# K and V in four transfers of 4 MB each, two heads per softmax, weights in the K and V buffers

## The chip, the cores and the metric

The kernel runs on one core of a Trainium2 chip. The metric is the device time of one execution in microseconds (us); the median of several runs counts.

## The reference

One decode step: attention of two tokens over a cached window, times a gate from a small dense network, plus the input. Cut to what matters:

```python
# x (2,1,448); k_cache, v_cache (2,8,8192,256); wq (448,4096); wo (4096,448)
# w1 (448,1792); w2 (1792,448); all bf16
W = 2048                                    # the last 2048 positions
xn = layernorm(x)
q = (xn @ wq) as 16 heads of 256            # two query heads for each K/V head
k, v = k_cache[:, :, -W:], v_cache[:, :, -W:]   # 8 heads, repeated twice
p = softmax(q k^T / 16)
s = (p v, heads side by side) @ wo
g = silu(relu(xn @ w1) @ w2)
return x + s * g
```

## The kernel before

Almost all bytes are K and V: 8 heads, each 2 MB of K and 2 MB of V for both batches, 33.5 of 44.1 MB. They come in sixteen transfers, one for a head's K or V: partition p = 2i + b holds 32 positions of batch b, a row of 32 x 256 values or 16 KB in one piece (`kv_src`, L175). wq (3.7 MB), w1 and w2 (1.6 MB each) come ahead of them, wo (3.7 MB) after them, in pieces of 16, 11, 4 and 1 of its 32 j-slices.

The program lists instructions by hand for each engine (`_Prog.op`, `_Prog.dma`); an instruction waits for those named in its `deps`, and each engine works through its own list in order. All the large transfers stand in the list of the sync engine (SP), so that one whose buffer is not free holds up those behind it. There are three buffers for K, three for V, two for the transposed K (`kt`), and own buffers for the weights (`wqo` for wq and later wo, `w1_sb`, `w2_sb`). `pump` (L504) puts a load into SP's list as soon as the step that frees its buffer has been listed.

A head k goes through these steps:

- `do_qbd`: POOL puts the head's queries into a block layout, four copies.
- `do_T(k, c)`, c = 0 to 3: VectorE (DVE) transposes a quarter of K in blocks of 32x32 words (L344).
- `do_S(k, c)`: TensorE (PE) multiplies that quarter with the queries, four matmuls of 512 columns into the bank `sbk`; at c = 0 a matmul of `wrow` with `wcol` first fills the bank with a large negative mask.
- the chain of the softmax: `ch_max` (DVE, the maximum of each row), `ch_rmT` (PE, transposes it), `ch_mrow` (DVE, the maximum over the rows of a query, negated), `ch_bias` (PE), `ch_bsb` and `ch_exp` (ScalarE, ACT), `ch_pt` (DVE, transposes the weights), `ch_sum` (PE) and `ch_rs` (DVE, 1/sum).
- `do_PV(k, q)`, q = 0 to 3: PE, 16 matmuls of 512 columns with V, four at a time side by side; `do_osb` (ACT) scales by 1/sum; `do_oT` (PE) and `do_at` (DVE) put the result into place.

The lists are written as a software pipeline (L441 to L471): the T and S of head k are interleaved with the chain of head k - 1 and the PV of head k - 2. After the last head its chain and the last three PV follow. Ahead of all this stand `do_q` (queries from wq), `do_H`, `do_hT` and `do_F` (the dense network; its gate `do_gate` after the T of head 0). At the end `at2` (L538) is made, and 32 x 4 matmuls with wo follow (L541), waiting at the first j of each piece for its landing; then two operations on DVE and the transfer of the output.

PE's matmuls are recorded by one helper, so L253 stands for nearly all of them; they are told apart by their tiles (`sbk` scores, `obk` PV and q, `fbk` the dense network and wo).

Of the kernel before, what the change touches and what calls it, by code (L numbers as in the profile page):

```python
# [74 lines left out]
def bass_recurrent_scan__sliding_block_cached__dense_activation_relu__decode_kernel(  # L75
# [31 lines left out]
    QW = 16 + 8 * 128  # L107
# [3 lines left out]
    with es:  # L111
# [19 lines left out]
        fold16 = named("fold16", [128, 16], BF)  # L131
# [19 lines left out]
        rm = [named(f"rm{i}", [128, 1], F32) for i in range(2)]  # L151
        mrow = [named(f"mrow{i}", [128, 128], F32) for i in range(2)]
# [3 lines left out]
        rs = named("rs", [128, NPAIR], F32)  # L156
# [4 lines left out]
        wqo = named("wqo", [128, 32 * D], BF)  # L161
        assert SLOTS * HC <= 32 * D
# [20 lines left out]
        last_T, last_PV = {}, {}  # L183
# [12 lines left out]
        d_wq = pr.dma(SP, wqo[:, 0:SLOTS * HC], wq_src)  # L196
        d_w1 = pr.dma(SP, w1_sb[:, :], w1_src)
        d_w2 = pr.dma(SP, w2_sb[:, :].rearrange("p (hf f) -> p hf f", hf=2), w2_src)
# [10 lines left out]
        p_mr = [pr.op(POOL, lambda e, t=t: e.memset(t[0:1, :], 0.0)) for t in mrow][-1]  # L209
        p_wr = pr.op(POOL, lambda e: e.memset(wrow[0:2, :], 0.0))  # L210
# [11 lines left out]
        for e2 in range(2):  # L222
# [10 lines left out]
            view(wrow, 0, [[16, 8], [2, 2], [1, 2]], n=2), view(ident, 0, [[0, 8], [1, 2], [0, 2]], n=2)), [p_wr, p_id])  # L233
        v_wc = pr.op(DVE, lambda e: e.tensor_scalar(
            out=view(wcol, 0, [[2, 256], [1, 2]], n=2), in0=view(ident, 0, [[0, 256], [1, 2]], n=2),
# [9 lines left out]
        def fold16_op(e):  # L245
            with nc.allow_low_precision("zeros and ones"):
                return e.tensor_reduce(out=fold16[:, :], in_=view(ident, 0, [[1, 16], [16, 8]]), axis=AX.X, op=ALU.add)
        v_f16 = pr.op(DVE, fold16_op)
        v_gs = pr.op(DVE, lambda e: e.tensor_copy(
            view(gsum, 0, [[4, 32], [1, 4]]), view(fold16, 0, [[0, 32], [1, 4]])), [v_f16])  # L250
# [14 lines left out]
        def do_q():  # L265
            deps = [d_wq, v_xr, a_z[0]]
            for s in range(SLOTS):
                for i in range(4):
                    lo = s * HC + i * 512
                    o = pr.op(PE, mm(obk[0][32 * i:32 * i + 4, :], xr[:, 4 * s:4 * s + 4], wqo[:, lo:lo + 512],  # L270
                                     s == 0, s == SLOTS - 1, tile_position=(0, 32 * i)), deps)
                    deps = []
            st["q_mm"] = o
            for par in range(2):
                v = pr.op(DVE, lambda e, par=par: e.tensor_scalar(  # L275
                    out=view(kt[1], 128 * par, [[256, 8], [32, 4], [1, 32]]),
                    in0=view(obk[0], par, [[64, 8], [0, 4], [2, 32]]),
                    scalar1=SCALE, scalar2=None, op0=ALU.mult), [o])
            st["osb", -2] = v
            deps = [v, p_id]  # L280
            for h in range(2):
                for cp in range(8):
                    n = 8 * h + cp
                    o = pr.op(PE, mm(nbk[:, 16 * n:16 * n + 16], kt[1][:, 128 * n:128 * n + 128],
# [7 lines left out]
        def do_qbd(k):  # L292
            deps = [st["qall"], p_qz, st.get(("S", k - 2))]
            for a in range(4):
                st["qbd", k] = pr.op(POOL, lambda e, a=a: e.tensor_copy(  # L295
                    view(qbd[k % 2], 16 + 32 * a, [[2, 2], [128, 8], [1, 2]], n=32, p0=32 * a),
                    view(qall, 32 * k, [[16, 2], [2, 8], [1, 2]], n=32, p0=32 * a)), deps)
                deps = []

        def do_H(u):  # L300
            deps = [d_w1, a_z[2], st.get("fbk"), st.get("h_n")]
            for s in range(SLOTS):
                lo = s * FC + u * (FC // 2)
                o = pr.op(PE, mm(fbk[0:4, 0:FC // 2], xr[:, 4 * s:4 * s + 4], w1_sb[:, lo:lo + FC // 2],
# [14 lines left out]
        def do_F():  # L319
            deps = [d_w2, st["hT"]]  # L320
            for f in range(14):
                for i in range(4):
                    lo = f * D + i * NCOL
                    o = pr.op(PE, mm(fbk[32 * i:32 * i + 17, 0:NCOL], h_sb[:, f:f + 17],
                                     w2_sb[:, lo:lo + NCOL],
# [15 lines left out]
        def do_T(k, c):  # L341
            src, dst = words(kbuf[k % NKB]), words(kt[k % 2])
            deps = [d_k[k], st.get(("S", k - 2)), st["qT"]] if c == 0 else []
            st["T", k, c] = pr.op(DVE, lambda e: e.transpose(  # L344
                view(dst, 32 * c, [[128, NT], [1, 32]]), view(src, 32 * c, [[128, NT], [1, 32]])), deps)
            if c == 3:
                last_T[k] = st["T", k, c]

        def do_S(k, c):
            bank, t = sbk[k % 2], kt[k % 2]  # L350
            if c == 0:
                pr.op(PE, mm(bank[:, :], wrow[0:2, :], wcol[0:2, :], True), [v_wr, v_wc, st.get(("exp", k - 2))])
            deps = [st["T", k, c]] + ([st["qbd", k]] if c == 0 else [])
            for par in range(2):
                for h in range(2):
                    w = 16 + (2 * c + par) * 128 - 16 * h
                    st["S", k] = pr.op(PE, mm(bank[:, :], qbd[k % 2][:, w:w + 128],
                                              view(t, 256 * h + 64 * c + par, [[512, NT // 2], [2, 32]]),
                                              False, c == 3 and par == 1 and h == 1), deps)
                    deps = []  # L360

        def ch_max(k):
            st["rm", k] = pr.op(DVE, lambda e: e.tensor_reduce(  # L363
                out=rm[k % 2][:, :], in_=sbk[k % 2][:, :], axis=AX.X, op=ALU.max),
                [st["S", k], st.get(("rmT", k - 2))])
# [6 lines left out]
        def ch_mrow(k):  # L372
            st["mrow", k] = st["mbk"] = pr.op(DVE, lambda e: e.tensor_reduce(  # L373
                out=view(mrow[k % 2], 0, [[16, 8], [1, 4]], n=1), in_=view(mbk, 0, [[0, 8], [1, 4], [16, 8]], n=1),
                axis=AX.X, op=ALU.max, negate=True), [st["rmT", k], p_mr, st.get(("bias", k - 2))])
# [14 lines left out]
        def ch_pt(k):  # L390
            st["pt", k] = pr.op(DVE, lambda e: e.transpose(pt[k % 2][:, :], e_sb[k % 2][:, :]),  # L391
                                [st["exp", k], last_PV.get(k - 2)])
# [8 lines left out]
        def do_PV(k, q):  # L401
            bank, src, p = obk[k % 2], vbuf[k % NVB], pt[k % 2]
            deps = [d_v[k], st["pt", k], a_z[1], st.get(("osb", k - 2))] if q == 0 else []
            for n in range(4 * q, 4 * q + 4):
                i = n % 4
                st["PV", k] = pr.op(PE, mm(bank[32 * i:32 * i + 20, :], p[:, 32 * n:32 * n + 20],
                                          src[:, 512 * n:512 * n + 512],
                                          q == 0, q == 3, tile_position=(0, 32 * i)), deps)
                deps = []
            if q == 3:  # L410
                last_PV[k] = st["PV", k]

        def do_osb(k):
            st["osb", k] = pr.op(ACTE, lambda e: e.activation(  # L414
                o_sb[k % 2][:, :], obk[k % 2][:, :], ACT.Copy, scale=rs[:, k:k + 1]),
                [last_PV[k], st["rs", k], st.get(("oT", k - 2))])

        def do_oT(k):
            deps = [st["osb", k], v_fold, st["nbk"]]
            for dhi in range(2):  # L420
                for t2 in range(2):
                    lo = 256 * t2 + 128 * dhi
                    o = pr.op(PE, mm(nbk[:, 4 * dhi:4 * dhi + 4], o_sb[k % 2][:, lo:lo + 128],
                                     fold[:, 16 * t2:16 * t2 + 4], dhi == 0 and t2 == 0, dhi == 1 and t2 == 1), deps)
# [3 lines left out]
        def do_at(k):  # L428
            for b in range(2):
                st["at", k] = st["nbk"] = pr.op(DVE, lambda e, b=b: e.tensor_tensor(  # L430
                    out=view(at_exp, 128 * b + 16 * k, [[4, 2], [8, 2], [1, 4]]),
                    in0=view(nbk, 2 * b, [[4, 2], [1, 2], [0, 4]]),
                    in1=view(qmask, 0, [[0, 2], [0, 2], [1, 4]]), op=ALU.mult), [st["oT", k], v_qm])

        steps = []

        def add(fn, *a):
            if 0 <= a[0] < NPAIR:
                steps.append((fn, a))

        for k in range(NPAIR):  # L441
            c, p, o = k - 1, k - 2, k - 3
            add(do_qbd, k)
            add(do_T, k, 0)
            add(ch_max, c)
            add(do_S, k, 0)
            add(ch_rmT, c)
            add(do_T, k, 1)
            add(ch_mrow, c)
            add(do_oT, o)  # L450
            add(do_at, o)
            add(do_T, k, 2)
            if k < NPAIR - 1:
                add(do_PV, p, 0)
            add(do_S, k, 1)
            add(ch_bias, c)
            add(ch_bsb, c)
            add(ch_exp, c)
            if k < NPAIR - 1:
                add(do_PV, p, 1)  # L460
            add(do_T, k, 3)
            add(do_S, k, 2)
            if k < NPAIR - 1:
                add(do_PV, p, 2)
            add(ch_pt, c)
            add(ch_sum, c)
            add(ch_rs, c)
            add(do_S, k, 3)
            if k < NPAIR - 1:
                add(do_PV, p, 3)  # L470
                add(do_osb, p)  # L471
        x, y, z = NPAIR - 3, NPAIR - 2, NPAIR - 1
# [113 lines left out]
```

## Time and profile before

| | |
|---|---|
| median of 3 runs | 111.65 us (111.58 to 112.1) |
| the profiled execution, its own time | 111.46 us |
| its span in the profile | 110.2 us |
| HBM read | 44.11 MB, 400 GB/s over the span |
| busy, share of the span | PE 64%, DVE 57%, PE weight loads 26%, ACT 17%, POOL 9% |
| mean granted TensorE clock | 0.864 |

Rows of the timeline read: start in us from the span's start, duration in us, engine, line, operation, output<-inputs, shapes, count, and in brackets how long the engine was idle before and what ended that. In section 2 of the page each digit is one fortieth of the span (2.755 us), in tenths.

### The profile page before, as it was taken

The page shows a single profiled execution, that of the slowest core. Times are in us where ns is not written, and L with a number is a line of the kernel's source. Part 1 is how long each engine was busy: PE and PEld are TensorE (multiplying, and loading weights), DVE is VectorE, ACT ScalarE, POOL GpSimd, SP SyncE. Part 2 cuts the span into 40 slices and gives each one's busy share as a digit, 9 for nine tenths or more (in the row PEclk, how much of TensorE's full clock was granted, in tenths as well). Part 3 has the DMA queues.
Part 4 walks back from the last instruction along what each step waited for, and adds up shares of the span by engine and source line. Part 5 has one row for each costly group of instructions (what it writes and reads, how often), then busy time and mean ns, then how long its engine had stood idle before and what let it go on. Part 6 is the DMA issues. An engine that isn't in the chain of part 4 may idle for free.

```text
span 110.2 us, 1454 instructions
## 1 busy us (share of the span) xinstructions
PE 70.2 (64%) x594; PEld 28.4 (26%) x594; DVE 63.3 (57%) x107; ACT 18.7 (17%) x40; POOL 10.2 (9%) x48
## 2 busy tenths in 40 slices
PE   0010746759948509994994895399979977834551
PEld 0000203134213202332331341133234432321540
DVE  2164057249999248739943990785499996221001
ACT  2970000000003000221032032003103220602000
POOL 6700000500020200011002002000200000000000
PEclk9999998599999965699579999655999999997555
DMA  6898999999999999999999999999999999999940
GB/s 167 354 480 356 433 410 461 428 434 428 422 428 434 422 434 422 434 422 437 411 428 422 434 422 434 422 434 422 434 422 434 411 440 416 440 419 416 406 162 1
DMA packets 3473, 44.19 MB, mean 401 GB/s; under 512 B 394, under 2 KB 524, under 8 KB 908
## 3 DMA queue, kind: packets, MB, share of 16 engines
q1 hardware_dynamic: 3440, 44.11, 94.8%
q8 instruction: 4, 0.07, 0.2%
q10 hardware_dynamic: 28, 0.01, 0.0%
q14 instruction: 1, 0.01, 0.0%
HBM read 44.11 MB, written 0.00 MB: 400 GB/s over the span
## 4 chain that ended last, share of the span: by engine, by line
DMA 63%; PE 19%; DVE 14%; SPq 2%; issue 1%
DMA kbuf<-in_A_k_cache_dram 37%; DMA wqo<-in_A_wo_dram 16%; DMA wqo<-in_A_wq_dram 10%; DVE kt L344 8%; PE sbk L253 6%; PE fbk L253 6%; PE obk L253 5%; DVE kt L275 2%; SPq L36 2%; DVE h_n L307 1%; PE nbk L253 1%; DVE rm L363 1%; PE mbk L253 1%; DVE tmp L549 0%; DVE h_sb L316 0%
## 5 line engine op out<-in xcount | busy, mean ns | idle before, releaser
L253 PE MATMUL sbk<-kt,qbd 128*128 128x512 bf16 x128 | 37.8, 422 | 14.7 <-DVE kt L344 14.5
L344 DVE STREAM_TRANSPOSE kt<-kbuf 128x1024 f32<-128x1024 f32 x32 | 38.3, 1218 | 11.2 <-DMA kbuf<-in_A_k_cache_dram 11.2
L253 PEld LDWEIGHTS sbk<-kt,qbd 128*128 128x128 bf16 x128 | 11.0, 106 | 32.1 <-DVE kt L344 20.8
L295 POOL COPY qbd<-qall 32x32 bf16<-32x32 bf16 x32 | 6.5, 204 | 68.8 <-PE sbk L253 53.1
L253 PE MATMUL obk<-vbuf,pt 128*20 128x512 bf16 x128 | 11.9, 410 | 1.5 <-DMA vbuf<-in_A_v_cache_dram 1.5
L382 ACT ACTIVATE bias<-mbk 128x1 f32<-128x1 f32 x8 | 1.4, 170 | 43.2 <-PE mbk L253 43.2
L414 ACT ACTIVATE o_sb<-obk,rs 128x512 bf16<-128x512 f32 x8 | 5.5, 686 | 18.5 <-PE obk L253 18.5
L391 DVE STREAM_TRANSPOSE pt<-e_sb 128x512 bf16<-128x512 bf16 x8 | 5.5, 683 | 3.0 <-ACT e_sb L386 3.0
L386 ACT ACTIVATE e_sb<-sbk,bias 128x512 bf16<-128x512 f32 x8 | 5.5, 687 | 0.3
L363 DVE TENSOR_REDUCE rm<-sbk 128x1 f32<-128x512 f32 x8 | 5.3, 657 | 0.5 <-PE sbk L253 0.5
L275 DVE TENSOR_SCALAR kt<-obk 128x1024 bf16<-128x1024 f32 x2 | 2.4, 1220 | 5.3 <-PE obk L253 5.3
L253 PE MATMUL obk<-wqo,xr 128*4 128x512 bf16 x28 | 3.2, 624 | 3.5 <-DMA wqo<-in_A_wq_dram 3.5
L253 PE MATMUL mbk<-ident,xg 2*128 2x2 bf16 x7 | 0.3, 163 | 7.9 <-DVE xg L223 7.9
L430 DVE TENSOR_TENSOR at_exp<-nbk,qmask 128x16 bf16<-128x16 f32 x16 | 1.9, 158 | 5.8 <-PE nbk L253 5.8
L253 PE MATMUL fbk<-wqo,at 128*17 128x112 bf16 x128 | 3.4, 296 | 2.9 <-DMA wqo<-in_A_wo_dram 2.9
L253 PEld LDWEIGHTS obk<-vbuf,pt 128*20 128x20 bf16 x128 | 2.9, 89 | 7.5 <-issue 4.9
L253 PE MATMUL fbk<-w_sb,xr 128*4 128x448 bf16 x14 | 4.2, 460 | 0.7 <-DVE h_n L307 0.7
L253 PEld LDWEIGHTS mbk<-one_f,mrow 1*128 1x128 f32 x16 | 2.9, 224 | 4.6 <-DVE kt L344 2.5
L373 DVE TENSOR_REDUCE mrow<-mbk 1x32 f32<-1x256 f32 x8 | 3.1, 386 | 1.3 <-PE mbk L368 1.3
L549 DVE TENSOR_TENSOR tmp<-fbk,g_sb 128x112 f32<-128x112 f32 x1 | 0.3, 273 | 6.1 <-PE fbk L253 6.1
L253 PEld LDWEIGHTS fbk<-wqo,at 128*17 128x17 bf16 x128 | 2.8, 129 | 3.3 <-issue 1.8
L253 PE MATMUL mbk<-one_f,mrow 1*128 1x1 f32 x16 | 3.5, 288 | 0.0
(64 smaller groups left out, 44.5 us busy)
## 6 DMA issues: line engine op xcount, KB each, us to landing
kbuf<-in_A_k_cache_dram SPq DMA_DIRECT2D x8, 2048.0 KB, 21.5
vbuf<-in_A_v_cache_dram SPq DMA_DIRECT2D x8, 2048.0 KB, 18.6
wqo<-in_A_wq_dram SPq DMA_DIRECT2D x1, 3584.0 KB, 11.0
w_sb<-in_B_w_dram SPq DMA_DIRECT2D x2, 1568.0 KB, 16.0
wqo<-in_A_wo_dram SPq DMA_DIRECT2D x1, 1792.0 KB, 15.7
wqo<-in_A_wo_dram SPq DMA_DIRECT2D x1, 1232.0 KB, 18.0
wqo<-in_A_wo_dram SPq DMA_DIRECT2D x1, 448.0 KB, 18.6
wqo<-in_A_wo_dram SPq DMA_DIRECT2D x1, 112.0 KB, 18.4
```

The source lines that it names most:

```text
L36: o = _Op(eng, lambda e: e.dma_start(dst, src), [d for d in deps if d is not None], True)
L253: return lambda e: e.matmul(out_ap, lhsT=lhsT, rhs=rhs, start=start, stop=stop, skip_group_check=True, **kw)
L275: v = pr.op(DVE, lambda e, par=par: e.tensor_scalar(out=view(kt[1], 128 * par, [[256, 8], [32, 4], [1, 32]]), in0=view(obk[0], par, [[64, ...
L295: st["qbd", k] = pr.op(POOL, lambda e, a=a: e.tensor_copy(view(qbd[k % 2], 16 + 32 * a, [[2, 2], [128, 8], [1, 2]], n=32, p0=32 * a), view ...
L344: st["T", k, c] = pr.op(DVE, lambda e: e.transpose(view(dst, 32 * c, [[128, NT], [1, 32]]), view(src, 32 * c, [[128, NT], [1, 32]])), deps)
L363: st["rm", k] = pr.op(DVE, lambda e: e.tensor_reduce(out=rm[k % 2][:, :], in_=sbk[k % 2][:, :], axis=AX.X, op=ALU.max), [st["S", k], st.ge ...
L373: st["mrow", k] = st["mbk"] = pr.op(DVE, lambda e: e.tensor_reduce(out=view(mrow[k % 2], 0, [[16, 8], [1, 4]], n=1), in_=view(mbk, 0, [[0, ...
L382: st["bsb", k] = st["mbk"] = pr.op(ACTE, lambda e: e.activation(bias[k % 2][:, :], mbk[:, 128:129], ACT.Copy), [st["bias", k]])
L386: st["exp", k] = pr.op(ACTE, lambda e: e.activation(e_sb[k % 2][:, :], sbk[k % 2][:, :], ACT.Exp, bias=bias[k % 2][:, 0:1], accum_out=ssum ...
L391: st["pt", k] = pr.op(DVE, lambda e: e.transpose(pt[k % 2][:, :], e_sb[k % 2][:, :]), [st["exp", k], last_PV.get(k - 2)])
L414: st["osb", k] = pr.op(ACTE, lambda e: e.activation(o_sb[k % 2][:, :], obk[k % 2][:, :], ACT.Copy, scale=rs[:, k:k + 1]), [last_PV[k], st[ ...
L430: st["at", k] = st["nbk"] = pr.op(DVE, lambda e, b=b: e.tensor_tensor(out=view(at_exp, 128 * b + 16 * k, [[4, 2], [8, 2], [1, 4]]), in0=vi ...
```

## The change

- K and V come in four transfers each of 4 MB: heads k and k + 4 of both batches. Partition p = 4i + g holds 64 positions of one of the four, a row of 32 KB.
- There are two buffers for K, two for V and one `kt`. wq lies in the second V buffer, w1 and w2 in the first, wo goes into the first K buffer once round 2 has been transposed. `load_v(0)` waits for the last matmul of `do_F`, `load_v(1)` for that of q, wo for `T(2, 7)`.
- A round k has eight T and eight S steps (of the same size as before; `c, gh = divmod(e, 2)`), one softmax for the two heads, and 32 PV matmuls. With one `kt`, `T(k, e)` waits for `S(k-1, e)`.
- `ch_mrow` has a second DVE operation; `do_qbd` has eight copies on POOL, `do_at` four products on DVE.
- The list's order is plainer: the T and S of rounds 0 and 1, with the chain of round 0 between those of round 1; then `chain(1, 0)` (the chain of round 1 with the PV of round 0 in it), T and S of round 2, `chain(2, 1)`, T and S of round 3, `chain(3, 2)`, PV of round 3.
- wo comes in pieces of 17, 9, 4 and 2.

The core of the diff:

```diff
-    NT = W // 64
+    NT = W // 32
-    NPAIR = HKV
+    NQ = HKV // 2
-    NKB = 3
-    NVB = 3
-    WO_PARTS = [16, 11, 4, 1]
+    WO_PARTS = [17, 9, 4, 2]
...
-        wqo = named("wqo", [128, 32 * D], BF)
-        w1_sb = named("w1_sb", [128, SLOTS * FC], BF)
-        w2_sb = named("w2_sb", [128, 14 * D], BF)
-        kbuf = [named(f"kbuf{i}", [128, ROW], BF) for i in range(NKB)]
-        vbuf = [named(f"vbuf{i}", [128, ROW], BF) for i in range(NVB)]
-        kt = [named(f"kt{i}", [128, ROW], BF) for i in range(2)]
+        kbuf = [named(f"kbuf{i}", [128, ROW], BF) for i in range(2)]
+        vbuf = [named(f"vbuf{i}", [128, ROW], BF) for i in range(2)]
+        kt = named("kt", [128, ROW], BF)
+        wq_sb, w12, wo_sb = vbuf[1], vbuf[0], kbuf[0]
...
         def kv_src(k, cache):
-            return cache[:, k, SK - W:SK, :].rearrange("b (i t) d -> i b (t d)", t=NT)
+            return cache.rearrange("b h s d -> (b h) s d")[k::NQ, SK - W:SK, :].rearrange("g (i t) d -> i g (t d)", t=NT)
...
         def load_k(k):
-            d_k[k] = pr.dma(SP, kbuf[k % NKB][:, :], kv_src(k, A_k_cache), [last_T.get(k - NKB)])
+            d_k[k] = pr.dma(SP, kbuf[k % 2][:, :], kv_src(k, A_k_cache), [st.get(("T", k - 2, 7))])
         def load_v(k):
-            d_v[k] = pr.dma(SP, vbuf[k % NVB][:, :], kv_src(k, A_v_cache), [last_PV.get(k - NVB)])
+            d_v[k] = pr.dma(SP, vbuf[k % 2][:, :], kv_src(k, A_v_cache),
+                            [(st["F"], st["q_mm"])[k] if k < 2 else st["PV", k - 2]])
...
-        def do_T(k, c):
-            src, dst = words(kbuf[k % NKB]), words(kt[k % 2])
-            deps = [d_k[k], st.get(("S", k - 2)), st["qT"]] if c == 0 else []
-            st["T", k, c] = pr.op(DVE, lambda e: e.transpose(
-                view(dst, 32 * c, [[128, NT], [1, 32]]), view(src, 32 * c, [[128, NT], [1, 32]])), deps)
+        def do_T(k, e):
+            c, gh = divmod(e, 2)
+            src, dst = words(kbuf[k % 2]), words(kt)
+            lo = 128 * (NT // 2) * gh + 32 * c
+            deps = [st.get(("S", k - 1, e))] + ([d_k[k], st["qT"]] if e == 0 else [])
+            st["T", k, e] = pr.op(DVE, lambda e: e.transpose(
+                view(dst, lo, [[128, NT // 2], [1, 32]]), view(src, lo, [[128, NT // 2], [1, 32]])), deps)
...
         def ch_mrow(k):
-            st["mrow", k] = st["mbk"] = pr.op(DVE, lambda e: e.tensor_reduce(
-                out=view(mrow[k % 2], 0, [[16, 8], [1, 4]], n=1), in_=view(mbk, 0, [[0, 8], [1, 4], [16, 8]], n=1),
-                axis=AX.X, op=ALU.max, negate=True), [st["rmT", k], p_mr, st.get(("bias", k - 2))])
+            v = st["mbk"] = pr.op(DVE, lambda e: e.tensor_reduce(
+                out=mx8[k % 2][0:1, :], in_=view(mbk, 0, [[1, 8], [8, 16]], n=1),
+                axis=AX.X, op=ALU.max, negate=True), [st["rmT", k]])
+            st["mrow", k] = pr.op(DVE, lambda e: e.tensor_copy(
+                view(mrow[k % 2], 0, [[8, 16], [1, 8]], n=1), view(mx8[k % 2], 0, [[0, 16], [1, 8]], n=1)),
+                [v, st.get(("bias", k - 2))])
...
+        def chain(k, pv=None):
+            ch_max(k)
+            ch_rmT(k)
+            ch_mrow(k)
+            ch_bias(k)
+            ch_bsb(k)
+            ch_exp(k)
+            if pv is not None:
+                for q in range(8):
+                    do_PV(pv, q)
+                do_osb(pv)
+            ch_pt(k)
+            ch_sum(k)
+            ch_rs(k)
+            if pv is not None:
+                do_oT(pv)
+                do_at(pv)
+
+        load_k(0)
+        load_k(1)
         do_q()
         do_H(0)
         do_H(1)
         do_hT()
         do_F()
+        load_v(0)
+        do_qbd(0)
+        do_qbd(1)
+        for e in range(8):
+            do_T(0, e)
+            do_S(0, e)
+            if e == 4:
                 do_gate()
+        load_k(2)
+        load_v(1)
...
+        load_k(3)
+        chain(1, 0)
+        load_v(2)
+        do_qbd(2)
+        for e in range(8):
+            do_T(2, e)
+            do_S(2, e)
+        chain(2, 1)
+        load_v(3)
+        do_qbd(3)
+        for e in range(8):
+            do_T(3, e)
+            do_S(3, e)
+        chain(3, 2)
+        for q in range(8):
+            do_PV(3, q)
+        do_osb(3)
+        do_oT(3)
+        do_at(3)
...
-            d_wo.append((j0, pr.dma(SP, wqo[:, j0 * D:(j0 + n) * D], wo_src[:, j0 * D:(j0 + n) * D], [st["q_mm"]])))
+            d_wo.append((j0, pr.dma(SP, wo_sb[:, j0 * D:(j0 + n) * D], wo_src[:, j0 * D:(j0 + n) * D], [st["T", 2, 7]])))
```

More of the change, by code (lines that the diff above doesn't have):

```diff
@@ L130, in bass_recurrent_scan__sliding_block_cached__dense_activation_relu__decode_kernel @@
         wcol = named("wcol", [128, 512], BF)
-        fold16 = named("fold16", [128, 16], BF)
+        fold8 = named("fold8", [128, 8], BF)
         qmask = named("qmask", [128, 4], F32)
@@ L151, in bass_recurrent_scan__sliding_block_cached__dense_activation_relu__decode_kernel @@
         rm = [named(f"rm{i}", [128, 1], F32) for i in range(2)]
+        mx8 = [named(f"mx8{i}", [128, 8], F32) for i in range(2)]
         mrow = [named(f"mrow{i}", [128, 128], F32) for i in range(2)]
@@ L292, in do_qbd @@
         def do_qbd(k):
-            deps = [st["qall"], p_qz, st.get(("S", k - 2))]
+            deps = [st["qall"], p_qz, st.get(("S", k - 2, 7))]
             for a in range(4):
[L295 to L298, printed above, removed]
+                for b in range(2):
+                    st["qbd", k] = pr.op(POOL, lambda e, a=a, b=b: e.tensor_copy(
+                        view(qbd[k % 2], 24 + 32 * a + 4 * b, [[2, 2], [128, 8], [1, 2]], n=32, p0=32 * a),
+                        view(qall, 32 * k + 16 * b, [[128, 2], [2, 8], [1, 2]], n=32, p0=32 * a)), deps)
+                    deps = []
         def do_H(u):
@@ L422, in do_oT @@
                     lo = 256 * t2 + 128 * dhi
-                    o = pr.op(PE, mm(nbk[:, 4 * dhi:4 * dhi + 4], o_sb[k % 2][:, lo:lo + 128],
-                                     fold[:, 16 * t2:16 * t2 + 4], dhi == 0 and t2 == 0, dhi == 1 and t2 == 1), deps)
+                    o = pr.op(PE, mm(nbk[:, 8 * dhi:8 * dhi + 8], o_sb[k % 2][:, lo:lo + 128],
+                                     fold[:, 8 * t2:8 * t2 + 8], dhi == 0 and t2 == 0, dhi == 1 and t2 == 1), deps)
                     deps = []
@@ L429, in do_at @@
             for b in range(2):
[L430 to L471, printed above, removed]
@@ L513, in bass_recurrent_scan__sliding_block_cached__dense_activation_relu__decode_kernel @@
-        pump()
+                for h in range(2):
+                    st["at", k] = st["nbk"] = pr.op(DVE, lambda e, b=b, h=h: e.tensor_tensor(
+                        out=view(at_exp, 128 * b + 64 * h + 16 * k, [[4, 2], [8, 2], [1, 4]]),
+                        in0=view(nbk, 4 * b + 2 * h, [[8, 2], [1, 2], [0, 4]]),
+                        in1=view(qmask, 0, [[0, 2], [0, 2], [1, 4]]), op=ALU.mult), [st["oT", k], v_qm])
+        def chain(k, pv=None):
[15 more added lines that the diff above has]
+                do_at(pv)
```

149 lines of the change are left out of this document (60 added, 89 removed).

## The prediction

> **What bounds the kernel now.** I read the page's slices and chain first, then the waits for landings in the timeline, then the timeline of the last 18 us.
>
> ```profile
> span 110.2 us, 1454 instructions
> PEclk9999998599999965699579999655999999997555
> DMA  6898999999999999999999999999999999999940
> DMA 63%; PE 19%; DVE 14%; SPq 2%; issue 1%
> ```
>
> The DMA row is full from the second slice to the last but two: the transfers never run dry. PEclk shows that the TensorE clock falls to half now and then, which matters below. The waits for landings say what the stream's pace is (column one is the time; the bracket names what was waited for):
>
> ```profile
> 30.37 1.25 DVE L344 STREAM_TRANSPOSE kt<-kbuf 128x1024 f32<-128x1024 f32 x1 [0.25 <-DMA kbuf<-in_A_k_cache_dram]
> ...
> 40.00 1.25 DVE L344 STREAM_TRANSPOSE kt<-kbuf 128x1024 f32<-128x1024 f32 x1 [3.44 <-DMA kbuf<-in_A_k_cache_dram]
> ...
> 49.80 1.25 DVE L344 STREAM_TRANSPOSE kt<-kbuf 128x1024 f32<-128x1024 f32 x1 [1.48 <-DMA kbuf<-in_A_k_cache_dram]
> ...
> 59.65 1.25 DVE L344 STREAM_TRANSPOSE kt<-kbuf 128x1024 f32<-128x1024 f32 x1 [1.84 <-DMA kbuf<-in_A_k_cache_dram]
> ...
> 79.22 1.25 DVE L344 STREAM_TRANSPOSE kt<-kbuf 128x1024 f32<-128x1024 f32 x1 [0.88 <-DMA kbuf<-in_A_k_cache_dram]
> ...
> 98.83 1.04 PE L253 MATMUL obk<-vbuf,pt 128*20 128x512 bf16 x16 [1.52 <-DMA vbuf<-in_A_v_cache_dram]
> ```
>
> From 40.00 to 98.83 twelve transfers of 2 MB landed: 9.80 us for two. 40.00, 49.80 and 59.65 are a V and a K apart, 79.22 to 98.83 a K and three V. VectorE waits for K each time, so compute keeps up. The end is the landing of wo and what follows it:
>
> ```profile
> 99.93 0.69 ACT L414 ACTIVATE o_sb<-obk,rs 128x512 bf16<-128x512 f32 x1 [3.27 <-PE obk L253]
> ...
> 100.67 0.27 PE L253 MATMUL nbk<-fold,o_sb 128*128 128x4 bf16 x4 [0.80 <-ACT o_sb L414]
> 100.97 0.26 DVE L430 TENSOR_TENSOR at_exp<-nbk,qmask 128x16 bf16<-128x16 f32 x2 [3.37 <-PE nbk L253]
> ...
> 101.56 0.23 DVE L538 CAST at<-mbk 128x64 bf16<-128x64 f32 x1 [0.33 <-PE mbk L253]
> ...
> 103.22 1.67 PE L253 MATMUL fbk<-wqo,at 128*17 128x112 bf16 x64 [1.70 <-DMA wqo<-in_A_wo_dram]
> ...
> 106.08 1.71 PE L253 MATMUL fbk<-wqo,at 128*17 128x112 bf16 x64 [1.19 <-DMA wqo<-in_A_wo_dram]
> 107.85 0.27 DVE L549 TENSOR_TENSOR tmp<-fbk,g_sb 128x112 f32<-128x112 f32 x1 [6.06 <-PE fbk L253]
> ```
>
> TensorE waits for the first wo piece until 103.22 and for the second until 106.08, then runs the last 16 j without a wait, 0.107 us per j. From its end (107.79) to the end of the span are 2.4 us that the change leaves alone. So a change pays only if the stream ends sooner, and costs only if compute no longer fits beneath it.
>
> **The stream.** The bytes are the same; the rows of K and V grow from 16,384 to 32,768 bytes, and eight transfers replace sixteen. What a longer row brings is bounded by three stretches of the DMA view (packets, MB, share of 16 engines): 5 to 10 us (wq, rows of 28,672 bytes), 20 to 95 us (K and V), 11 to 18.5 us (w1 and w2, 12,544 and 6,272).
>
> ```profile
> q1 hardware_dynamic: 70, 2.01, 93.1%
> ```
> ```profile
> q1 hardware_dynamic: 2195, 32.03, 100.4%
> ```
> ```profile
> q1 hardware_dynamic: 413, 3.21, 101.1%
> ```
>
> Bytes by engine time (2.01 MB in 0.931 x 16 x 5 us, and so on) give 26.98, 26.59 and 26.46 KB per us: longer rows are a little quicker. A row of 28,672 bytes takes 1,063 ns, one of 16,384 takes 616 ns; the line through them puts 32,768 bytes at 1,212 ns. Against 2 x 616 that saves 20 ns a row, and against the pace of the landings (9.80/16 = 612.5 ns) 13 ns. An engine takes 8 rows of each transfer: 64 rows x 13 = 0.8 us by the last V, 1.3 by the other reckoning; a row that is cut in two underway saves 0. I take 0.8, since the landings are what the end hangs on; the range keeps 0 and 1.3.
>
> The rows also change places: neighbouring partitions held the two batches of one head (32 MiB apart) and now hold two heads of two batches (16 MiB apart). The Trainium skill ("DMA: Bandwidth & Descriptors", section on latency and other measured facts) says that tiles whose partition rows lie a large power of two apart are slow, 103 GB/s per direction at 4 and 8 MiB. That speaks against this change, but K and V of before lie so already and move 2 x 2.1 MB in 9.80 us, 428 GB/s. I keep the row's pace; the rule is a rival below.
>
> Same bytes, so each new landing is an old one less 0.1 us per 4 MB: K0 30.3, K1 39.8, V0 49.5, K2 59.3, V1 69, K3 78.6, V2 88.3, V3 98.0.
>
> **Does the queue stay full?** Each buffer now waits for its last reader, all on SP's one queue. V0 waits for do_F:
>
> ```profile
> 24.54 0.87 PE L253 MATMUL fbk<-w_sb,h_sb 128*17 128x112 bf16 x56 [0.46 <-DVE h_sb L316]
> ```
>
> Done at 25.4, with K1 still to stream until about 39. K2 (after T(0,7), about 41) has V0 ahead of it until 49; V1's wait is long over; K3 (after T(1,7), about 54) has until 68; V2 (after PV(0)) about 60 against 78; V3 (after PV(1), about 76) against 88; wo stands behind V3, its own wait (T(2,7), 70) over. Each is 7 us or more ahead. Costs nothing; should compute fall 7 us behind, this cover goes too.
>
> **Compute beneath the stream.** A round has the same eight T and 32 S matmuls as two old ones, one softmax for two, and 32 PV matmuls:
>
> ```profile
> 28.96 0.85 DVE L334 RECIPROCAL tmp<-ea 128x112 f32<-128x112 f32 x1
> ...
> 82.57 2.35 DVE L344 STREAM_TRANSPOSE kt<-kbuf 128x1024 f32<-128x1024 f32 x2
> ...
> 83.85 1.04 PE L253 MATMUL sbk<-kt,qbd 128*128 128x512 bf16 x4
> ...
> 91.86 0.12 DVE L399 RECIPROCAL rs<-nbk 128x1 f32<-128x1 f32 x1
> ...
> 92.47 0.69 DVE L363 TENSOR_REDUCE rm<-sbk 128x1 f32<-128x512 f32 x1 [0.49 <-PE sbk L253]
> 93.22 0.27 PE L368 MATMUL mbk<-ident_f,rm 128*1 128x128 f32 x1 [0.78 <-DVE rm L363]
> ...
> 93.42 1.04 PE L253 MATMUL obk<-vbuf,pt 128*20 128x512 bf16 x16
> 93.53 0.41 DVE L373 TENSOR_REDUCE mrow<-mbk 1x32 f32<-1x256 f32 x1 [0.36 <-PE mbk L368]
> ...
> 94.39 0.38 PE L253 MATMUL mbk<-one_f,mrow 1*128 1x1 f32 x2
> ...
> 95.30 0.69 ACT L386 ACTIVATE e_sb<-sbk,bias 128x512 bf16<-128x512 f32 x1
> ...
> 96.14 0.70 DVE L391 STREAM_TRANSPOSE pt<-e_sb 128x512 bf16<-128x512 bf16 x1
> ```
>
> T: 8 x 1.175 = 9.4 us; S trails by one group, 1.1. Then, now in a row and with T(k+1) behind them on VectorE: max 0.7, its transposition 0.35, mrow 0.45, the added copy (not in the trace; 128 values on one partition, between rs at 0.12 and mrow at 0.41: 0.2), bias 0.45, PV 2.1, osb 0.75, oT 0.3, four at-products 0.5 (bsb, exp and pt run beside PV): 5.8 us. One round is 9.4 + 1.1 + 5.8 = 16.3 us against 19.6 of transfers. In round 1 the chain of round 0 sits between the T (max, mrow, copy, pt, rs: 2.1, about 1 of waits). T0 30.3 to 41 with do_gate's 1.3 (the reciprocal's 0.85 and two small ones); T1 to 53.5, chain(1,0) to 60.5; T2 about 1 us after K2's landing, to 70; chain(2,1) to 77; T3 at K3's 78.6, to 88.0; chain(3,2) to 95.0. PV(3) waits for V3 at 98.0: 3 us of cover. do_qbd doubles to eight copies a round, where POOL waits for most of the span:
>
> ```profile
> 19.30 1.94 POOL L295 COPY qbd<-qall 32x32 bf16<-32x32 bf16 x8 [14.57 <-DVE qall L289]
> ```
>
> Two sets there end at 23.2, before T0: nothing (later sets wait for S two rounds back, long done). The edits to the masks and to `fold8` lie before wq's landing; nothing either, and 0.2 us if that cover went. The half clock is the risk, since a wait for K precedes each S stretch:
>
> ```profile
> 41.30 1.89 PE L253 MATMUL sbk<-kt,qbd 128*128 128x512 bf16 x4 [3.90 <-DVE kt L344]
> ```
> ```profile
> 39.00:43.00 4.00, 1.70 (x5) 0.54 (x5) 2.97 (x3) 0.00 (x0) 0.00 (x0) 0.52 0.98 418
> 43.00:47.00 4.00, 4.00 (x19) 1.33 (x18) 2.69 (x3) 0.75 (x2) 0.00 (x0) 0.63 1.02 434
> ```
>
> After an idle 3.9 us a group of four takes 1.89, not 1.04, and the clock (sixth figure after the stretch's length) is back inside the next stretch, which is busy throughout. Three groups so cost about 2 us a round: chain(3,2) ends at 95 to 97, still below V3.
>
> **The tail.** V3 98.0; PV(3) has 32 matmuls, 2.1 instead of 1.04; at four products instead of two, 0.25: `at2` stands 3.0 + 1.3 = 4.3 us after V3, at 102.3. wo after V3: 17 pieces for 16, 4.35 x 17/16 = 4.6, so 102.6; nine for eleven, 2.9 x 9/11 = 2.4, so 105.0; the last lands like this in before, issued at 89.0:
>
> ```profile
> wqo<-in_A_wo_dram SPq DMA_DIRECT2D x1, 112.0 KB, 18.4
> ```
> ```profile
> L36 SPq DMA_DIRECT2D wqo<-in_A_wo_dram x4: 432/432/595, 87.4 to 89.0; - x4
> ```
>
> so 107.4, and 0.8 sooner now: 106.6. TensorE: 105.0 + 15 x 0.107 = 106.6, then the last two j, 106.9. Before: 107.79. Sum: the stream -0.8, better pieces -0.1, doubled PV and at hidden (cover 0.3 us up to the first piece, and up to at2 = 106.9 - 3.4 = 103.5 for the end). Span 109.3; the profiled execution of 111.46 becomes 110.6; the median of the runs is 0.19 above it: **110.8 us**, 0.8% below 111.65. About 0.5% is what a measurement of this kernel tells from no change.
>
> **Rivals.** *Nothing left* (0.21): rows of 32 KB save nothing, or TensorE is at half clock for PV(3) after its wait for V3. That stage then takes 1.6 more (8 groups of about 0.2), at2 103.9, end 107.3, which eats half the gain. 111.2 to 111.7. For it: the clock fell before the last stage already (the 5s at PEclk's end). Against: TensorE is busy nearer to V3 than to K.
>
> *Compute becomes the bound* (0.21), the slower side: T(k+1) stands behind chain(k), so a late softmax moves all that follows. Its place is S3 and chain(3,2); it decides once chain(3,2) ends past 99.2 (V3 plus the 1.2 of cover), i.e. with 4 us more than I reckon: six of eight groups at 1.89 (0.72 each over T), or 1 us on each of four chains. All of round 3 at half clock: S3 ends at 78.6 + 1.2 + 15.1 = 94.9, chain with PV(2) at half clock 7.4, PV(3) 3.7, the rest to at2 2.2, wo 3.4: 111.6 instead of 106.9, 115.5 us in all. Half of that, 113. For it: PEclk's 5s. Against: those stretches never last over three slices, 8 us, and end where TensorE is busy.
>
> *The row pitch* (0.04): rows 16 MiB apart, four by four, hinder one another more than pairs 32 MiB apart. Each tenth off the 428 GB/s costs 78.4/9 = 8.7 us: 119.5 for one tenth. By the page of the Trainium skill named above, 33.5 MB at 103 GB/s, an estimate of 360 us. Against: 428 at the pitch of before.
>
> **How the numbers follow.** Forecast 0.54 (110.3 to 111.0 by itself), nothing left 0.21, compute 0.21, pitch 0.04. A gain over 0.5% is the forecast's case, 0.54; within 0.5%, nothing left and the mildest of compute, 0.23; slower 0.23. The range starts at the 1.3 us of the busy times, 110.2, and reaches to compute's half price, 113.0.
>
> **What would show it.** Right: two K starts on VectorE 19.4 us apart (59.3, 78.6) with a wait for DMA; DMA full to the end; PV(3) waiting for V3 near 98; last matmuls ending near 106.9. Wrong: T2 or T3 waiting for an at-product instead of K; S groups of 1.9 us through a whole round; first wo matmul waiting for at2; GB/s below 428.

## The result and the profile after

The changed kernel runs in 110.58 us (median of 6 runs, 110.48 to 110.73) against 111.67 us of the kernel before: a ratio of 0.990, 95% interval 0.988 to 0.992. Forecast were 110.8 us. The span went from 110.2 to 109.3 us. From the page after:

```profile
span 109.3 us, 1328 instructions
...
PEclk9999999999556999999996559999959999955559
DMA  6898999999999999999999999999999999999940
...
DMA 70%; DVE 12%; PE 12%; SPq 3%; issue 1%
```

The DMA row is as full as it was: the waits for buffers that stand in SP's list cost nothing. The chain that ended last is even more of a chain of transfers (70%, before 63%). The timeline of VectorE shows the rounds (start, duration, and in brackets what was waited for):

```profile
59.03 9.13 DVE L343 STREAM_TRANSPOSE kt<-kbuf 128x1024 f32<-128x1024 f32 x8 [1.11 <-DMA kbuf<-in_A_k_cache_dram]
...
74.86 0.41 DVE L433 TENSOR_TENSOR at_exp<-nbk,qmask 128x16 bf16<-128x16 f32 x4 [0.57 <-PE nbk L249]
```
```profile
78.39 9.13 DVE L343 STREAM_TRANSPOSE kt<-kbuf 128x1024 f32<-128x1024 f32 x8 [3.11 <-DMA kbuf<-in_A_k_cache_dram]
```

T2 and T3, the transposition steps of rounds 2 and 3, each begin when their K has landed, 19.36 us apart; the same bytes took 19.6 before. Chain(2,1) ends 3.1 us before K3 is there. The tail, from the timeline of all engines:

```profile
93.59 0.42 DVE L433 TENSOR_TENSOR at_exp<-nbk,qmask 128x16 bf16<-128x16 f32 x4 [0.57 <-PE nbk L249]
...
98.14 3.59 PE L249 MATMUL obk<-vbuf,pt 128*16 128x512 bf16 x32 [4.59 <-DMA vbuf<-in_A_v_cache_dram]
...
103.58 0.22 DVE L521 CAST at<-mbk 128x64 bf16<-128x64 f32 x1 [0.33 <-PE mbk L249]
...
103.86 3.12 PE L249 MATMUL fbk<-kbuf,at 128*17 128x112 bf16 x128 [0.32 <-DVE at L521]
106.70 0.11 PEld L249 LDWEIGHTS fbk<-kbuf,at 128*17 128x17 bf16 x8 [0.23 <-DMA kbuf<-in_A_wo_dram]
107.03 0.28 DVE L532 TENSOR_TENSOR tmp<-fbk,g_sb 128x112 f32<-128x112 f32 x1 [3.23 <-PE fbk L249]
```

V3 landed at 98.1 (the last V of before at 98.8). PV(3) took 3.59 us, not 2.1, so `at2` was ready at 103.80, not 102.3. The first matmul with wo therefore waited for `at2` and not for a piece of wo, which the prediction names as a sign of being wrong. The 128 matmuls then ran nearly without a wait: only the last two j waited 0.23 us for the last piece, until 106.70. The table by stretches says why PV(3) was slow (the sixth figure after a stretch's length is the granted clock):

```profile
79.60:82.40 2.80, 2.71 (x7) 1.00 (x8) 2.80 (x4) 0.00 (x0) 0.00 (x0) 0.50 0.89 386
82.40:88.60 6.20, 6.05 (x27) 2.08 (x24) 5.12 (x5) 0.00 (x0) 0.00 (x0) 1.00 1.00 433
94.00:98.10 4.10, 0.00 (x0) 0.00 (x0) 0.00 (x1) 0.00 (x0) 0.00 (x0) 0.75 0.87 372
98.10:101.80 3.70, 3.59 (x32) 0.98 (x32) 0.00 (x0) 0.02 (x1) 0.00 (x0) 0.50 0.98 416
```

TensorE had nothing to do from 94.0 to 98.1, the clock fell in that stretch (0.75 on the mean), and PV(3) ran at half clock. The same happened to the first S of round 3 (0.50), which was back at 1.00 after 2.8 us of work.

### The profile page after: what moved, and what is told of

Read it like the earlier page. It is cut to its first block, busy times and chain, and to the rows that moved or that the text cites. A ratio compares the mean times of both kernels' runs of the same rounds, so it can differ in the third digit from the quotient of the medians.

```text
span 109.3 us, 1328 instructions
## 1 busy us (share of the span) xinstructions
PE 63.9 (58%) x554; PEld 26.0 (24%) x554; DVE 57.6 (53%) x95; ACT 12.4 (11%) x24; POOL 9.0 (8%) x45
## 4 chain that ended last, share of the span: by engine, by line
DMA 70%; DVE 12%; PE 12%; SPq 3%; issue 1%
DMA kbuf<-in_A_k_cache_dram 42%; DMA kbuf<-in_A_wo_dram 28%; DVE kt L343 10%; PE sbk L249 9%; SPq L36 3%; PE obk L249 2%; DVE tmp L331 1%; DVE rm L361 1%; PE mbk L249 0%; PE nbk L249 0%; PE fbk L249 0%; DVE mx L371 0%; DVE tmp L532 0%; PE mbk L366 0%; DVE out_sb L534 0%
## 5 line engine op out<-in xcount | busy, mean ns | idle before, releaser
L249 PE MATMUL obk<-vbuf,pt 128*16 128x512 bf16 x128 | 9.3, 442 | 4.6 <-DMA vbuf<-in_A_v_cache_dram 4.6
L249 PE MATMUL obk<-vbuf,xr 128*4 128x512 bf16 x28 | 3.2, 626 | 3.8 <-DMA vbuf<-in_A_wq_dram 3.8
L392 DVE STREAM_TRANSPOSE pt<-e_sb 128x512 bf16<-128x512 bf16 x4 | 2.8, 711 | 4.7 <-ACT e_sb L387 4.7
L249 PEld LDWEIGHTS obk<-vbuf,pt 128*16 128x16 bf16 x128 | 3.1, 98 | 8.5 <-DMA vbuf<-in_A_v_cache_dram 4.7
L361 DVE TENSOR_REDUCE rm<-sbk 128x1 f32<-128x512 f32 x4 | 2.7, 682 | 4.0 <-PE sbk L249 4.0
L249 PE MATMUL fbk<-vbuf,xr 128*4 128x448 bf16 x14 | 4.3, 461 | 0.7 <-DVE h_n L304 0.7
L416 ACT ACTIVATE o_sb<-obk,rs 128x512 bf16<-128x512 f32 x4 | 2.7, 687 | 11.1 <-PE obk L249 11.1
L249 PE MATMUL fbk<-kbuf,at 128*17 128x112 bf16 x128 | 3.1, 282 | 0.4 <-DVE at L521 0.3
L249 PEld LDWEIGHTS fbk<-kbuf,at 128*17 128x17 bf16 x128 | 2.7, 128 | 0.7 <-DVE at L521 0.4
L387 ACT ACTIVATE e_sb<-sbk,bias 128x512 bf16<-128x512 f32 x4 | 2.7, 687 | 0.1
## 6 DMA issues: line engine op xcount, KB each, us to landing
vbuf<-in_B_w_dram SPq DMA_DIRECT2D x2, 1568.0 KB, 16.2
```

The lines of the kernel that those rows point to most:

```text
L249: return lambda e: e.matmul(out_ap, lhsT=lhsT, rhs=rhs, start=start, stop=stop, skip_group_check=True, **kw)
L361: st["rm", k] = pr.op(DVE, lambda e: e.tensor_reduce(out=rm[k % 2][:, :], in_=sbk[k % 2][:, :], axis=AX.X, op=ALU.max), [st["S", k, 7], st ...
L387: st["exp", k] = pr.op(ACTE, lambda e: e.activation(e_sb[k % 2][:, :], sbk[k % 2][:, :], ACT.Exp, bias=bias[k % 2][:, 0:1], accum_out=ssum ...
L416: st["osb", k] = pr.op(ACTE, lambda e: e.activation(o_sb[k % 2][:, :], obk[k % 2][:, :], ACT.Copy, scale=rs[:, k:k + 1]), [st["PV", k], st ...
```

## The experiments

The theory: the end hangs on the stream, which is quicker because rows are longer; compute is hidden. Rivals: the gain is of another origin (fewer transfers, fewer softmaxes, the pieces of wo); compute binds; the distance of the rows in HBM matters. Medians are compared with runs of the kernel before on the same chip.

### Rows of 16 KB in the changed kernel

```diff
-            d_k[k] = pr.dma(SP, kbuf[k % 2][:, :], kv_src(k, A_k_cache), ...)
+            for h in range(2):
+                lo, hi = h * ROW // 2, (h + 1) * ROW // 2
+                d_k[k, h] = pr.dma(SP, kbuf[k % 2][:, lo:hi], kv_src(k, A_k_cache)[:, :, lo:hi], ...)
...                                                    # V alike
```

> The changed kernel, but every 4 MB load of K or V is two transfers of 2 MB, each with the first or second half of all 128 rows: rows of 16 KB and sixteen transfers, as before the change; buffers, softmax and order of work as changed. If the gain is that of the longer rows (1,213 against 613 ns a row and its half, 64 long rows for each engine, about 0.8 us), it goes: about 111.4 us, and K of round 3 is transposed some 0.6 us later than 78.4. If the gain came from anything else in the change (half the softmaxes, less work on VectorE, the wo pieces), the time stays at 110.6.

Measured (e1): 110.91 us against 111.56 (0.994, 0.993 to 0.996). Neither expectation held: about 0.65 us of the gain stay with rows as short and transfers as many as before; against 110.54 of a run with long rows in the same series ("The old pieces of wo"), long rows in half as many transfers are worth 0.37 us. The DMA view from 30 to 90 us (packets, MB, share of 16 engines) of the kernel before, of this run and of the changed kernel:

```profile
q1 hardware_dynamic: 1754, 25.59, 100.3%
```
```profile
q1 hardware_dynamic: 1770, 25.85, 100.7%
```
```profile
q1 hardware_dynamic: 886, 25.89, 100.2%
```

In bytes by engine time (25.59 MB in 1.003 x 960 us, and so on) these are 26.58, 26.74 and 26.91 KB per us. Rows of the same 16 KB moved 0.6% quicker in the changed kernel than before, which over 78 us of K and V is 0.5 us; doubling the row gave another 0.6%.

Short stretches in which only rows of K or V begin give the time of one row (a row is counted whole in the stretch where it begins). The kernel before and this run, 45 to 47 us, and the changed kernel, 34 to 37 us:

```profile
q1 hardware_dynamic: 53, 0.87, 101.9%
```
```profile
q1 hardware_dynamic: 51, 0.84, 97.4%
```
```profile
q1 hardware_dynamic: 46, 1.51, 116.2%
```

That is 615 ns for a row of 16 KB in the kernel before (1.019 x 16 x 2 us for 53 rows), 611 ns in this run, and 1,213 ns for a row of 32 KB. So a long row saves some 10 ns against two short ones of 611, by estimate 0.6 us over an engine's 64 rows, and the 4 ns between 615 and 611 make 0.5 us over 128 rows. Both ways of counting give 1.0 to 1.1 us in all; the share of the length is 0.4 us by the times of the runs and 0.6 by the rows.

The end of this run hangs on something else than the end of the changed kernel:

```profile
98.36 3.59 PE L254 MATMUL obk<-vbuf,pt 128*16 128x512 bf16 x32 [4.35 <-DMA vbuf<-in_A_v_cache_dram]
...
104.07 3.08 PE L254 MATMUL fbk<-kbuf,at 128*17 128x112 bf16 x128 [0.32 <-DVE at L526]
```

No matmul waits for a piece of wo here. The end follows from V3's landing, PV(3) at half clock and the matmuls behind it, so a little of the 0.37 us may be the half clock and not the stream.

### Rows of 32 KB in sixteen transfers

```diff
+            for h in range(2):
+                d_k[k, h] = pr.dma(SP, kbuf[k % 2][64 * h:64 * h + 64, :], kv_src(k, A_k_cache)[16 * h:16 * h + 16], ...)
```

> The changed kernel, but every 4 MB load of K or V is two transfers of 2 MB, one for partitions 0 to 63 and one for 64 to 127: sixteen transfers as before the change, rows of 32 KB as after. If the length of the rows makes the gain, it stays: 110.6 us. If the number of transfers makes it (a fixed cost for each of them), it goes: about 111.4 us.

Measured (e2): 191.59 us (1.720, 1.715 to 1.724). This answers another question than the one asked. From 30 to 90 us:

```profile
q1 hardware_dynamic: 489, 12.88, 101.6%
```

The DMA engines are as busy as ever and move half: 13.2 KB per us each. In this run a transfer to 64 neighbouring partitions had half the rate of one to 128. The Trainium skill ("SBUF — State Buffer", on the DMA port swizzle) says that partitions 0 to 63 reach only 8 of the 16 ports, and 64 to 127 the other 8; this run agrees, 13.2 against 26.9. So no run separates the number of transfers from the length of the rows. The row times above speak for the length, since the 10 ns are inside the rows. And the number isn't what sets the run before apart from the kernel before: both have sixteen.

### The old pieces of wo

```diff
-    WO_PARTS = [17, 9, 4, 2]
+    WO_PARTS = [16, 11, 4, 1]
```

> The changed kernel with wo in the pieces of before (16, 11, 4, 1). By the sum of the prediction the pieces bring 0.1 us: 110.7 us. By the trace after, TensorE starts on wo only at 103.9, when at2 is ready, and then runs 3.1 us nearly without a wait, so that the first three landings bind nothing: 110.6 us, no change.

Measured (e3): 110.54 us against 111.56 (0.991, 0.990 to 0.992). No gain from the new pieces shows, though 0.1 us is less than these medians can tell apart. Here PV(3) was at half clock for a part only:

```profile
97.89 2.92 PE L249 MATMUL obk<-vbuf,pt 128*16 128x512 bf16 x32 [3.55 <-DMA vbuf<-in_A_v_cache_dram]
...
102.93 1.68 PE L249 MATMUL fbk<-kbuf,at 128*17 128x112 bf16 x64 [0.32 <-DVE at L521]
105.10 1.73 PE L249 MATMUL fbk<-kbuf,at 128*17 128x112 bf16 x64 [0.50 <-DMA kbuf<-in_A_wo_dram]
```

The second piece was waited for, 0.5 us, and the end came at 106.83, much as with the new pieces. Behind that wait no other is seen: the second landing and 16 j after it, 0.108 us each at a granted clock of 0.50, close this run, as they closed the kernel before.

### TensorE kept at work before the last PV

```diff
         chain(3, 2)
+        for n in range(16):
+            pr.op(PE, mm(wbk[:, :], ident[:, :], e_sb[1][:, :], True, True), [])
```

> The changed kernel with 16 matmuls of 128x512 more on TensorE (on data at hand, into a bank that nothing reads) after the last oT of chain(3,2), where TensorE waits for V3. The clock should then be full in the last PV: 32 matmuls in about 1.9 us instead of 3.6, at2 at about 102.1 instead of 103.6. If the end of wo's stream binds, as the prediction has it, the end moves by less than 0.2 us (last landing 106.65, two j after it): 110.4 to 110.6 us. If the half clock in the last PV costs what the rival said, its 1.6 us show in part: 110.0 us or less.

Measured (e4): 110.68 us against 111.56 (0.992, 0.990 to 0.993).

```profile
98.03 1.90 PE L250 MATMUL obk<-vbuf,pt 128*16 128x512 bf16 x32 [0.29 <-DMA vbuf<-in_A_v_cache_dram]
...
101.75 0.23 DVE L524 CAST at<-mbk 128x64 bf16<-128x64 f32 x1 [0.31 <-PE mbk L250]
...
102.65 1.01 PE L250 MATMUL fbk<-kbuf,at 128*17 128x112 bf16 x68 [0.94 <-DMA kbuf<-in_A_wo_dram]
...
104.98 2.01 PE L250 MATMUL fbk<-kbuf,at 128*17 128x112 bf16 x60 [1.31 <-DMA kbuf<-in_A_wo_dram]
```

PV(3) is 1.7 us shorter, `at2` 1.8 sooner, and all of it turns into waits for wo (0.94 and 1.31): the end is 106.99, where it was 106.98. The half clock in PV(3) costs nothing in the changed kernel, because the landings of wo bind; but the 0.23 us that its last two j waited are all that was to spare.

### Compute made later, within and beyond its cover

```diff
         def ch_pt(k):
             st["pt", k] = ...
+            for n in range(3 if k >= 1 else 0):          # first run; second: 11 if k == 3 else 0
+                st["pt", k] = pr.op(DVE, lambda e: e.transpose(pt[k % 2][:, :], e_sb[k % 2][:, :]), [st["pt", k]])
```

> The changed kernel with three more transpositions of the weights (0.71 us each, with nothing of use in them) after ch_pt in the chains of rounds 1, 2 and 3: VectorE's chain is 2.2 us longer in each. By the prediction compute has cover in each round (the waits for K of 1.1 and 3.1 us and for V of 4.6 us in the trace after), so a delay of 2.2 us moves T2 by 1.1, T3 by 0.2 and PV(3) not at all: 110.6 us. If VectorE's order already binds the rounds, each 2.2 us shows: 113 us or more.

Measured (e5): 110.51 us against 111.54 (0.990, 0.989 to 0.992): nothing. T2 and T3 in that run:

```profile
59.56 9.12 DVE L343 STREAM_TRANSPOSE kt<-kbuf 128x1024 f32<-128x1024 f32 x8
...
78.51 9.13 DVE L343 STREAM_TRANSPOSE kt<-kbuf 128x1024 f32<-128x1024 f32 x8 [0.63 <-DMA kbuf<-in_A_k_cache_dram]
```

T2 now starts behind the at-products (0.5 later, no wait for K), T3 still waits for K. 2.2 us in each of the three rounds are hidden.

> The changed kernel with eleven more such transpositions in round 3 alone, 8.1 us: the weights are ready at about 100.5 instead of 92.4, past V3's landing at 98.1. By the prediction compute then sets the end: PV(3) 2.4 us later, and at2 was ready at 103.8 with TensorE at work without a pause from there to the end, so 2.4 us show in full: 113.0 us; if the clock is full in PV(3) then, 1.6 less: 111.4. If the end hung on the stream with much slack, it would stay near 110.6.

Measured (e6): 112.85 us against 111.54 (1.012, 1.010 to 1.015), 2.3 us over the changed kernel.

```profile
93.49 8.18 DVE L395 STREAM_TRANSPOSE pt<-e_sb 128x512 bf16<-128x512 bf16 x11
...
102.05 3.59 PE L249 MATMUL obk<-vbuf,pt 128*16 128x512 bf16 x32
...
107.73 1.75 PE L249 MATMUL fbk<-kbuf,at 128*17 128x112 bf16 x128 [0.32 <-DVE at L523]
109.54 0.28 DVE L534 TENSOR_TENSOR tmp<-fbk,g_sb 128x112 f32<-128x112 f32 x1 [1.86 <-PE fbk L249]
```

The total is close to the 113.0 expected, but by two errors that cancel. PV(3) came 3.9 us later, not 2.4: round 3 reached its softmax 1.0 later, and the last oT, which stands ahead of PV(3) on TensorE, waited for the reciprocal behind the transpositions. And the 128 matmuls with wo, all landed by now, took 1.75 us, not 3.12. The bound itself is shown: compute sets the end once it passes V3's landing by enough.

### Where the quicker 16 KB rows come from

The kernel before with the changed kernel's places in HBM, and the changed kernel (rows split) with those of before:

```diff
-            return cache[:, k, SK - W:SK, :].rearrange("b (i t) d -> i b (t d)", t=NT)
+            four = cache.rearrange("b h s d -> (b h) s d")[k % 4::4, SK - W:SK, :]
+            return four.rearrange("g (i h t) d -> h i g (t d)", h=2, t=NT)[k // 4]
```

> The kernel before, whose sixteen transfers take other rows of K and V: each 2 MB transfer has rows of 16 KB from four head-and-batch pairs (every second 16 KB of the rows that the changed kernel loads) instead of 64 neighbouring rows from each batch of one head; nothing else differs, and the scores are those of other positions. With rows of 16 KB in both, the changed kernel with split rows ran 0.6 us sooner than the kernel before. If the places in HBM from which rows come make that, this run gains it: about 111.0 us. If it comes from the rest of the change (half the softmaxes, less traffic of the engines beside the transfers, other buffers), it stays at 111.6.

> The changed kernel with each 4 MB load split in two of 2 MB with 16 KB rows, each half now taken as the kernel before takes it: the two batches of one head, 64 neighbouring rows of each; nothing else differs, and a partition's two halves belong to two heads, so that the scores are not the reference's. If the places in HBM make the remaining 0.6 us, it loses them: about 111.5 us. If the rest of the change makes them, it stays at 110.9.

Measured (x1, x2): 111.62 us against 111.54 (1.000, 0.999 to 1.001), and 110.94 (0.994, 0.993 to 0.995). Both rates go with the kernel, not with the places in HBM; from 30 to 90 us, x1 first:

```profile
q1 hardware_dynamic: 1756, 25.63, 100.4%
```
```profile
q1 hardware_dynamic: 1769, 25.84, 100.7%
```

Then the kernel before with its transfers in the changed order (two K, two V in turn), and with two buffers instead of three (`NKB` and `NVB` 2):

```diff
-        order = [("k", 0), ("k", 1)] ...
+        order = []
+        for c in "kk kk vv kk vv kk vv vv".replace(" ", ""):
+            order.append((c, sum(o[0] == c for o in order)))
```

> The kernel before with its sixteen transfers in the order in which the changed kernel with split rows has them: four K, then two V, two K and so on by twos, instead of a V and a K in turn; buffers, rows and compute as before. Rows of 16 KB move 25.85 MB between 30 and 90 us in the changed kernel with split rows, 25.59 in the kernel before. If the order makes that, this run moves 25.8 and ends near 111.0 us. If it is the number of buffers or the rest of the change, 25.6 and 111.5.

> The kernel before with two buffers of 16 KB for K and two for V instead of three each; order and compute as before, and transfers are issued later, some 4 us ahead of the stream. If three buffers in turn, or the number of transfers that stand in the queue, make 16 KB rows slower, this run moves 25.8 MB between 30 and 90 us and ends near 111.0 us, unless a transfer comes too late; if not, 25.6 and 111.5, or more where the stream runs dry.

Measured (x3, x4): 113.32 us (1.016, 1.012 to 1.020) and about 124 us (1.108, 1.104 to 1.113), against 111.65. In both the stream ran dry, so that the times say nothing of the rows. The first ran dry only near its end; from 30 to 90 us it still shows the old rate, so the order isn't it:

```profile
q1 hardware_dynamic: 1755, 25.61, 100.4%
```

The second stopped about 50 us in, so its time is inconclusive. It shows what the third buffer of before was for. Its rows say more. The kernel before from 20 to 23 us, then this run from 45 to 47 and from 83 to 85:

```profile
q1 hardware_dynamic: 79, 1.29, 100.6%
```
```profile
q1 hardware_dynamic: 51, 0.84, 98.0%
```
```profile
q1 hardware_dynamic: 51, 0.84, 97.4%
```

These are 611, 615 and 611 ns a row. In the kernel before, K of head 0 went into the first K buffer at 611 ns a row (20 to 23 us) and K of head 3 into the same buffer at 615 (45 to 47 us, shown above). With two buffers the rows were at 615 before the stream stopped and at 611 later. So the place of the buffer alone does not make the slower rows: they set in while the kernel runs, and they can go away again. What makes them, no run shows.

### Rows far apart in HBM

```diff
-            return ...[k::NQ, SK - W:SK, :].rearrange("g (i t) d -> i g (t d)", t=NT)
+            return ...[:, SK - W + 512 * k:SK - W + 512 * k + 512, :].rearrange("g (i t) d -> g i (t d)", t=NT)
```

> The changed kernel with each 4 MB load taken from all sixteen head-and-batch pairs, 512 positions of each, eight rows of 32 KB one after another for each pair: groups of eight partitions lie 4 MiB apart in HBM instead of four rows of neighbouring partitions 16 MiB apart; the scores are those of other positions. If a pitch of large powers of two between partitions slows a load, K and V stream at well below 428 GB/s here: at half of it 190 us, at the 103 GB/s of the Trainium skill an estimate of 360 us. If the pitch does nothing at this rate, as the rows of 1,213 ns suggest, 110.6 us.

> The run before this one (sixteen groups of eight rows of 32 KB, 192.9 us) with the groups 288 KB apart instead of 4 MiB: same sizes, same number of rows in a group, same places on chip, other rows of the caches, so that the scores are of other positions. If the distance of 4 MiB halved the rate, the rate is back here: 110.6 us. If it was the shape of the transfer (sixteen groups of eight, and which engine takes which rows), it stays at 193 us.

Measured (e7, e8b): 192.87 us (1.728, 1.725 to 1.731) and 192.27 us (1.721, 1.716 to 1.726). From 30 to 90 us, 4 MiB apart first:

```profile
q1 hardware_dynamic: 434, 12.65, 100.4%
```
```profile
q1 hardware_dynamic: 433, 12.62, 100.5%
```

Half the rate in both, so the distance of 4 MiB isn't the cause. What the two share is the shape of the source, sixteen groups of eight rows instead of 32 of four. That the eight rows are neighbours in HBM isn't slow by itself: so are all rows of wq, and they had the full rate (26.98 KB per us and engine in the kernel before). That the shape changes which engine takes which rows, and so how many of them write to one place on chip at a time, would fit the same half rate as with 64 partitions, but no run shows which engine took what. The first run alone would have looked like proof of the rule on pitch that the prediction weighs.

## Why the prediction was right

**The stream** was right in its end and wrong in its parts. V3 came at 98.1 (forecast 98.0), the wait for the second wo piece ended at 104.98 in a run that has one (105.0), the last j began at 106.70 (106.6), the end came at 106.98 (106.9). The term "64 rows x 13 = 0.8 us" is the step that was mis-sized. The long row was right, 1,213 ns (1,212). But 612.5 ns, the kernel's own pace, was taken for what any 16 KB row takes, and the whole difference was put down to length. With rows of 16 KB in the changed kernel a row took 611 ns, so the length gives 0.6 us by the rows and 0.37 by the times of the runs. The rest, 0.5 to 0.65 us, comes because rows of 16 KB are quicker there than in the kernel before. That the two parts came near the forecast sum is luck, and the second part is not explained. It isn't the places in HBM (x1, x2), not the order (x3), not the number of transfers (e1 has sixteen), not cover for compute (e5), and not the places of the buffers alone (the same one was filled at 611 and at 615 ns a row). Other differences of the two kernels, such as what the engines do beside the transfers, were not separated.

**The queue stays full**: right, DMA shows no gap; the places where waits were named (V0 for do_F, V3 for PV(1)) left none.

**Compute beneath the stream**: a round from T2's start to the last at-product took 16.2 us (16.3), the added copy 0.21 (0.2). T2 waited for K, where I had it 1 us late: T1 had fewer waits than reckoned. The half clock came where it was said to, in the first S after a wait, but S caught up: in round 3 its last group ended 1.1 us after the last T, as at full clock.

**The rivals**: the half clock in PV(3) happened, the case for "nothing left", at its full price for that stage (3.59 against 1.90). The reason given against it, that TensorE is busy nearer to V3 than to K, did not hold: it had been idle for 4.6 us. The end still did not move, by a narrow margin. The prediction allowed `at2` until 103.5; it came at 103.80, and 32 j at 0.107 us from there would have ended at about 107.2. They took 3.12 us instead of 3.4, at a clock of 0.61 on the mean, so that the last landing at 106.65 still closed the kernel. 0.107 us per j is about the pace at half clock and not one that holds whatever the clock: e6 shows 1.75 us for all 32 at full clock. Compute as the bound was shown to be real (e6): chain(3,2) ended 4.1 us before V3, where 3 were reckoned, and e5 took up 2.2 of them without loss. The pitch of 16 MiB did nothing, at 428 GB/s and more. The 103 GB/s that the Trainium skill ("DMA: Bandwidth & Descriptors", latency and other measured facts) states are for copies between tensors in HBM, and no run here shows that case.

**The tail**: from V3 to `at2` it took 5.7 us, not 4.3, and this was hidden only as far as said above. The -0.1 for the pieces did not show (e3).

## What to carry to other kernels

In a kernel bound by one stream, price every change of compute by the wait it falls into: 2.2 us a round, a whole stage at half clock (with 0.2 us to spare) and new pieces of wo moved nothing here, while 0.6% in the rate of rows moved the end. Rows of K and V of 32 KB instead of 16 are worth having but small, 0.4 to 0.6 of 111 us; a pace measured in one kernel isn't the pace of that row size in another. And test a suspected cause against a twin that has its shape without it: a slow run with rows 4 MiB apart proved nothing until the same shape at 288 KB was as slow.

## What the runs showed of the hardware that I had not expected

- A transfer to 64 neighbouring partitions ran at half the rate of one to 128: 13.2 against 26.9 KB per us and engine, 191.6 us in all.
- So did a transfer to all 128 whose source is sixteen groups of eight rows (13.1), with the groups 4 MiB or 288 KB apart, while 32 groups of four had the full rate.
- Small matmuls (112 columns) follow the clock too: 128 of them took 3.12 us at a clock of 0.61 on the mean, 0.23 us of waiting included, and 1.75 us at 1.00 in e6.
- 16 KB rows moved 26.58 KB per us and engine in one kernel and 26.74 in another, wherever they came from. Within the first kernel a row took 611 ns early on and 615 later, into the same buffer.
